# RWKV-7 attention and a hard-swish feed-forward on one core: whole-tile turns in place of half-tile turns

## The chip, the core and the metric

The kernel runs on one core of one Trainium2 chip. Its engines work side by side, each through its own queue in order: TensorE (PE for the matmuls, PEld for the loads of weights), VectorE (DVE), ScalarE (ACT), GpSimd (POOL) and SyncE (SP), which issues most of the DMAs. Matmuls write to PSUM, which the program here uses in eight banks of 512 fp32 columns by 128 partitions; DVE and ACT move results on to SBUF ("eviction"). The metric is device time in microseconds, the median of the runs. Lower is better.

## What is computed

First a recurrence with a state of 40 x 40 per head, for 4 batches, 8 heads, 768 steps; then its output, as 3072 rows of 320, goes through a feed-forward block with 2048 inner features. All of it is fp32.

```python
for t in range(S):                       # S = 768, D = 40
    y[:, :, t] = einsum('bhd,bhde->bhe', rt, state)
    Sa = einsum('bhde,bhe->bhd', state, at)
    state_decay = state * wt[:, :, None, :] - einsum('bhd,bhe->bhde', Sa, bt)
    state = state_decay + einsum('bhd,bhe->bhde', vt, kt)
# x = y as (B*S, H*D) = (3072, 320)
h = x @ w_in                             # (320, 2048)
g = h * clip(h + 3.0, 0.0, 6.0) / 6.0
return g @ w_out                         # (2048, 320)
```

## The kernel before

**Units.** The sequence is cut into blocks of 64 steps. A unit is one block of two batches with all 8 heads: its two batches lie on the two halves of the 128 partitions. There are 24 units in 6 groups of four. Within a block the recurrence is written as matrix products: A and B scaled by running products of the decays ("gam") and their inverses ("rgam"), a 64 x 64 triangular matrix F per head and batch, its inverse ("tinv"), and products with the state.

**Stages of a unit.** `prepare(i)` holds what needs no state: `w_stage` and `gam_stage` (running products of W and their inverses), `a_stage` and `b_stage` (A and B turned and scaled), `F`, `k_stage`, `factor_stage` (the inverse gammas turned back, with which K and B are scaled in their own layout), `e_stage`, `ev_stage`. `step(i)` holds the rest: `s_RT` and `s_VT` (R and V turned), `s_R`, `s_C`, `s_S` (the state turned), `s_U`, `s_UT`, `s_rS`, `s_sn` (the sums added to the state), `s_H`, `s_y`, and the moves of y into the layout of the feed-forward.

**Turns.** Inputs arrive with time on the partitions and are wanted with features there. A turn is a TensorE transpose: the data is the loaded weight, the identity is streamed through. `turn_pairs` (L416) turns a tensor in four transposes of 128 x 128 into one PSUM bank. `turn_halves` (L425) does it in eight transposes of 64 x 128, one for each half of the partitions and pair of heads. Each streams 64 columns of the identity, the two halves of the array work at the same time, and the results of the two halves lie in two banks, half a bank each; a second tensor shares these banks. The evictions then come in two instructions, one for each bank, over which `in_halves` and `parts_of` run. The flag `halves` chooses: it is set for units 8 to 23 in `prepare` (A, B and the inverse gammas) and for units 4 to 23 in `step` (R and V). W, K and the state are always turned whole.

**Order.** The order of the instructions on every engine is written out by hand. After a part for the first two groups comes the main loop (from L1280) over units 4 to 23. Each unit has four blocks; block m runs the stages that the lists `OWN_STAGES`, `AHEAD_STAGES` and `CLOSE_STAGES` set for the unit itself and for the one being prepared ahead (units 8 to 23, mostly five units ahead). Between the blocks, `feed` puts pieces of the feed-forward (`expand`, L961, and `contract`, L984) and steps of the inversion of F (`invert`, on DVE).

Inside a block `together` first issues the TensorE work of all stages in the order of the list `PRODUCTS`, then all evictions in the order of `RESULTS`, which also decides when the loads for later units are issued on SP. It counts banks: five are there for this work, and where the next product would need a sixth it closes the group early. A stage in `TURNS` takes a bank of its own; the others share pairs of banks while they have columns left.

```python
PRODUCTS = ["W", "S", "K", "RT", "VT", "A", "B", "factor",
            "y", "EV", "R", "C", "U", "UT", "rS", "sn", "H", "E", "F"]
TURNS = PRODUCTS[:3]
```

So in a typical unit the four blocks hold, on TensorE: W, RT, VT, y (of the unit before), EV; then S, A, B, R, C; then K, U, UT, rS, F; then factor, sn, H, E.

Of the kernel before, what the change touches and what calls it, by code (L numbers as in the profile page):

```python
# [11 lines left out]
ALU = mybir.AluOpType  # L12
AF = mybir.ActivationFunctionType
# [3 lines left out]
P = 128  # L17
BL = 64
HB = BL // 2
L = 32  # L20
SLOT = 64


def _ap(ap, extra, dims):

    return bass.AP(tensor=ap.tensor, offset=ap.offset + extra, ap=[list(ap.ap[0])] + dims)
# [3 lines left out]
def kernel(  # L30
# [42 lines left out]
    nc = tc.nc  # L73
    B, H, T, D = r.shape
    NG = T // (2 * BL)
    NPR = H // 2
    NP = B // 2
    NU = 2 * NP
# [16 lines left out]
    def bank(tag, shape, bufs):  # L95
        return ps.tile(shape, F32, name=tag, tag=tag, bufs=bufs)
# [3 lines left out]
    def ps_any(shape):  # L100
        tag, bufs = ring[0]
        ring.rotate(-1)
        return bank(tag, shape, bufs)
# [4 lines left out]
    def ps_pair(*dims):  # L108

        n = 1  # L110
        for d in dims:
            n *= d
        if shared[0] is None or shared[1] + n > 512:
            shared[:] = [ps_any([P, 512]) for _ in range(2)], 0
        at = shared[1]
        shared[1] += n
        views, step = [], n
        for d in dims:
            step //= d
            views.append([step, d])  # L120
        return [_ap(t[:], at, views) for t in shared[0]]
# [4 lines left out]
    ident = const.tile([P, P], F32, name="ident")  # L126
    nc.gpsimd.affine_select(
        out=ident[:], in_=ones, pattern=[[1, P]],
# [4 lines left out]
        out=ones[:, 0:BL], in_=ones[:, 0:BL], pattern=[[1, BL]],  # L133
# [3 lines left out]
        out=ones[BL:P, 0:BL], in_=ones[BL:P, BL:P], pattern=[[1, BL]],  # L137
# [271 lines left out]
    def following(i):  # L409

        if i < 2 * NU:

            return i + 2 if i % NU < NU - 2 or i % 2 == 0 else None
        return i + 1

    def turn_pairs(x):  # L416

        o = ps_any([P, NPR, P])
        for n in range(NPR):
            nc.tensor.transpose(out=o[:, n, :],  # L420
                                in_=x[:, 2 * n:2 * n + 2, :].rearrange("p s e -> p (s e)"),
                                identity=ident[:])
        return o

    def turn_halves(x):  # L425

        o = ps_pair(NPR, BL)
        for n in range(NPR):
            for q in range(2):
                nc.tensor.transpose(out=o[q][:, n, :],  # L430
                                    in_=x[half(q), 2 * n:2 * n + 2, :].rearrange("p s e -> p (s e)"),
                                    identity=ident[half(q), half(q)])
        return o

    def in_halves(x):
        return [x[:, :, half(q)] for q in range(2)]

    def turn_in(x, halves):

        return turn_halves(x) if halves else [turn_pairs(x)[:]]  # L440

    def parts_of(x, halves):
        return in_halves(x) if halves else [x[:]]

    def turned(name):
        return tmp.tile([P, NPR, P], F32, name=name, tag="turned", bufs=5)

    def half(i, n=SLOT):
        return slice(SLOT * i, SLOT * i + n)
# [20 lines left out]

    def prepare(i, F):
        n, o = i % NU, data[i]
        halves = i >= 2 * NU
        def w_stage():
            wt = turn_pairs(o["WN"])
            yield PE
# [27 lines left out]
            yield from ()  # L504

        def a_stage():
            x = turn_in(o["AN"], halves)
            yield PE
            rv = o["rg"][:].rearrange("p r (q i) -> p (r q) i", q=2)
            nc.vector.reciprocal(rv[:, :, HB:BL], o["prods"][:, :, 1, 1:HB + 1])  # L510
            at = o["at"] = grp.tile([P, NPR, P], F32, name="at", tag="at")
            for y, z, g in zip(parts_of(at, halves), x, parts_of(o["G"], halves)):
                nc.vector.tensor_tensor(out=y, in0=z, in1=g, op=ALU.mult)
            fetch("A", following(i))

        def b_stage():
            x = turn_in(o["BN"], halves)
            yield PE
            bt = o["bt"] = turned("bt")
            for y, z, g in zip(parts_of(bt, halves), x, parts_of(o["rg"], halves)):  # L520
                nc.vector.tensor_tensor(out=y, in0=z, in1=g, op=ALU.mult)

        def f_by_32():

# [38 lines left out]

        def factor_stage():

            if halves:
                rg = ps_pair(NPR, SLOT)
                for pr in range(NPR):
                    for s in range(2):
                        nc.tensor.transpose(out=rg[s][:, pr, :], in_=o["rg"][half(s), pr, :],  # L570
                                            identity=ident[half(s), half(s)])
            else:
                rg = ps_any([P, NPR, P])
                for pr in range(NPR):
                    nc.tensor.transpose(out=rg[:, pr, :], in_=o["rg"][:, pr, :], identity=ident[:])
            yield PE
            rgt = tmp.tile([P, H, D], F32, name="rgt", bufs=RGT)
            if halves:
                for s in range(2):
                    nc.scalar.activation(out=rgt[:, s::2], in_=rg[s][:, :, 0:D], func=AF.Copy)  # L580
            else:
                nc.scalar.activation(
                    out=rgt[:], in_=rg[:].rearrange("p r (s e) -> p (r s) e", s=2)[:, :, 0:D],
                    func=AF.Copy,
                )
            t = grp.tile([P, HD + WPAD], F32, name="KBt", tag="KBt", bufs=NU + 2)
            nc.gpsimd.memset(t[:, 2 * HD:], 0.0)
            for x, name in enumerate("KB"):
                o[name] = t[:, x * HD:x * HD + WPAD]
                nc.gpsimd.tensor_tensor(  # L590
                    out=o[name][:, 0:HD].rearrange("p (h e) -> p h e", h=H),
                    in0=o[name + "N"][:, :, 0:D], in1=rgt[:], op=ALU.mult,
                )
            if i > 2 * NU:
                fetch("V", i)
            for name in "BK":
                fetch(name, following(i))
# [137 lines left out]
    def step(i):  # L735

        n, o = i % NU, data[i]
        g, p = names[i]
        st, dec, VN = state[p], o["dec"], o["VN"]
        fresh = i < NP  # L740
        halves = i >= NU
        m = {}

        def s_RT():
            x = turn_in(o["RN"], halves)
            yield PE
            m["RT"] = turned("RT")
            for y, z in zip(parts_of(m["RT"], halves), x):
                nc.scalar.activation(out=y, in_=z, func=AF.Copy)  # L749
            fetch("R", i + 1, nc.scalar if i == 0 else None)  # L750
            if fresh:
                nc.gpsimd.tensor_copy(last_dec[p][:], dec[:, 1])
                return
            scale = tmp.tile([P, 2, NPR], F32, name="scale", bufs=2)
            nc.gpsimd.tensor_tensor(out=scale[:], in0=last_dec[p][:], in1=dec[:, 0], op=ALU.mult)
            nc.gpsimd.tensor_copy(last_dec[p][:], dec[:, 1])
            nc.vector.tensor_tensor(out=st[:, :, :, 0:D], in0=st[:, :, :, 0:D],
                                    in1=_ap(scale[:], 0, [[NPR, 2], [1, NPR], [0, D]]), op=ALU.mult)
# [16 lines left out]
                nc.vector.tensor_tensor(out=R[:, s], in0=rp[s], in1=o["EV"][:, s], op=ALU.add)  # L775

        def s_VT():
            x = turn_in(VN, halves)
            yield PE
            m["VT"] = turned("VT")  # L780
            for y, z in zip(parts_of(m["VT"], halves), x):
                nc.scalar.activation(out=y, in_=z, func=AF.Copy)

        def new_U():
            U = m["U"] = grp.tile([P, H, SLOT], F32, name="U", tag="U", bufs=1)
# [323 lines left out]
    n, cleared = 0, []  # L1109
# [48 lines left out]
    for line in PLAN:  # L1158
        plan.append([])
        while line:  # L1160
            i = line.popleft()
            if i != "T":
                i = int(i)
# [30 lines left out]
    for _ in range(18):  # L1194
# [10 lines left out]
    CLOSE_STAGES = [["W", "gam"], ["A", "B"], ["F", "K", "factor"], ["E"], ["EV"]]  # L1205


    PRODUCTS = ["W", "S", "K", "RT", "VT", "A", "B", "factor",
                "y", "EV", "R", "C", "U", "UT", "rS", "sn", "H", "E", "F"]
    RESULTS = ["RT", "y", "W", "gam", "VT", "EV", "R", "S", "C", "A", "B", "move", "move2",  # L1210
               "U", "UT", "rS", "F", "K", "sn", "H", "E", "factor"]
    TURNS = PRODUCTS[:3]
    WIDTH = {"R": NPR * D, "U": NPR * D, "sn": NPR * D, "EV": NPR * D}
    BLOCKS = 4

    def together(stages):
# [10 lines left out]

        for name in PRODUCTS:
            for stage in stages.get(name, []):
                if name in TURNS:  # L1230
                    need = 1
# [3 lines left out]
                if banks + need > 5:  # L1235
                    finish()
                    banks, need = 0, 1 if name in TURNS else 2
                banks += need
                rest = stage()
                next(rest)  # L1240
                begun.append((name, rest))
        begun.extend((name, stage()) for name in stages if name not in PRODUCTS
                     for stage in stages[name])
# [35 lines left out]
    m = 0  # L1279
# [59 lines left out]
```

## Time and profile before

| | |
|---|---|
| median of 3 runs | 840.49 us (839.77 to 842.09) |
| the profiled execution | 842.09 us |
| its span, first to last instruction | 840.4 us |
| TensorE matmul busy | 753.9 us (90%) |
| TensorE weight loads busy | 635.5 us (76%) |
| DVE / ACT / POOL busy | 549.1 / 322.6 / 158.2 us |
| granted TensorE clock, mean of the span | 0.937 |
| L992 and L968, the feed-forward's products | 234.6 and 198.1 us |
| half turns at L430 and L570 | 39.0 us in 704 instructions |

Busy times are of one execution. In rows of the timeline the first number is the start, the second the time from the first start to the last end of the group; matmuls overlap their followers, so the time that a group takes from TensorE is read from its start to the next group's start. "ident,R" in such a row names the streamed operand and then the weight; "64\*128" is the shape of the weight, "128x64" or "64x64" that of the streamed one. In rows of groups the number after the bar is the busy time in us and the mean of one instruction in ns, and after the next bar the idle time of the engine just before them.

### The profile page before, as it was taken

How to read it: one execution, taken by the hardware profiler on the slowest of the kernel's cores; microseconds unless marked ns; L12 is line 12 of the kernel's file. 1: busy time of each engine (PE TensorE's matmuls, PEld its weight loads, DVE VectorE, ACT ScalarE, POOL GpSimd, SP SyncE). 2: the span in 40 equal slices, each digit the busy share in tenths (PEclk: the TensorE clock that was granted, in tenths of full speed). 3: DMA queues.
4: the chain of work that ended last, by engine and by line, in shares of the span. 5: the costliest groups of instructions: out<-in, count | busy, mean ns of one | idle time of the engine just before them, and what ended most of it. 6: DMA issues, size and time to landing. Idle time of an engine off the chain costs nothing.

```text
span 840.4 us, 35835 instructions
## 1 busy us (share of the span) xinstructions
PE 753.9 (90%) x15832; PEld 635.5 (76%) x15832; DVE 549.1 (65%) x1112; ACT 322.6 (38%) x868; POOL 158.2 (19%) x307
## 2 busy tenths in 40 slices
PE   4722866898999998999999999999999999999998
PEld 3622766686877877888888888888888888888886
DVE  6989597887865769855589744699556675232211
ACT  1322654232265533454433545334553324322111
POOL 3231310222112230312230322022122102000000
PEclk9755576999999998999999999999999999999999
DMA  7573343331033331232321332231232101110000
GB/s 140 83 176 92 90 105 91 69 68 34 9 59 59 63 61 28 43 55 46 61 44 33 59 59 44 44 57 29 47 64 43 24 22 28 25 23 15 16 19 16
DMA packets 174218, 45.05 MB, mean 54 GB/s; under 512 B 157424, under 2 KB 172784, under 8 KB 174064
## 3 DMA queue, kind: packets, MB, share of 16 engines
q1 hardware_dynamic: 171920, 42.44, 25.7%
q8 instruction: 125, 2.05, 1.0%
q10 hardware_dynamic: 2144, 0.33, 0.2%
q14 instruction: 29, 0.24, 0.1%
HBM read 34.08 MB, written 3.93 MB: 45 GB/s over the span
## 4 chain that ended last, share of the span: by engine, by line
PE 73%; DVE 12%; issue 6%; ACT 2%; POOL 2%; DMA 2%; SPq 0%; POOLq 0%; DVEq 0%; ACTq 0%
PE o L992 23%; PE h L968 20%; PE h L973 5%; PE any L458 4%; PE any L888 3%; PE any L420 2%; PE any L430 2%; PE any L864 2%; PE any L770 1%; DVE prod L660 1%; PE any L809 1%; DVE parts L320 1%; DVE x L666 1%; PE any L830 1%; DVE score L467 1%
## 5 line engine op out<-in xcount | busy, mean ns | idle before, releaser
L992 PE MATMUL o<-wout,gt 128*128 128x320 f32 x768 | 234.6, 449 | 0.0
L968 PE MATMUL h<-xt,win 128*128 128x128 f32 x1536 | 198.1, 283 | 5.0 <-DVE gt L979 5.0
L968 PEld LDWEIGHTS h<-xt,win 128*128 128x128 f32 x1536 | 186.7, 196 | 13.9 <-DVE gt L979 5.7
L992 PEld LDWEIGHTS o<-wout,gt 128*128 128x128 f32 x768 | 139.3, 191 | 54.4 <-issue 1.4
L979 DVE SCALAR_TENSOR_TENSOR gt<-gt,h 128x512 f32<-128x512 f32 x96 | 61.3, 681 | 87.1 <-ACT gt L978 87.0
L978 ACT ACTIVATE gt<-h,three 128x512 f32<-128x512 f32 x96 | 60.8, 684 | 108.3 <-PE h L973 108.2
L903 POOL TENSOR_TENSOR yg<-ys,gam 128x512 f32<-128x512 f32 x24 | 41.4, 1726 | 182.9 <-DVE ys L900 125.5
L660 DVE TENSOR_TENSOR prod<-x 128x30 f32<-128x30 f32 (+9 forms) x180 | 61.9, 344 | 13.5 <-POOL x L651 8.1
L590 POOL TENSOR_TENSOR KBt<-K,rgt 128x320 f32<-128x320 f32 x24 | 21.2, 882 | 248.2 <-ACT rgt L580 213.2
L666 DVE TENSOR_TENSOR x<-x,prod 128x30 f32<-128x30 f32 (+9 forms) x180 | 63.3, 352 | 5.2
L873 DVE TENSOR_TENSOR state<-any,state 40x160 f32<-40x160 f32 x96 | 30.9, 321 | 47.5 <-PE any L458 26.0
L973 PE MATMUL h<-xt,win 64*128 64x128 f32 x768 | 55.8, 285 | 0.0
L467 DVE COPY_PREDICATED score<-mask,any 128x256 f32<-128x256 int32 x143 | 53.4, 437 | 1.7 <-PE any L458 1.1
L973 PEld LDWEIGHTS h<-xt,win 64*128 64x128 f32 x768 | 46.6, 187 | 5.2 <-issue 0.3
L495 DVE RECIPROCAL gam<-prods 128x256 f32<-128x256 f32 x24 | 41.5, 1741 | 13.4 <-POOL yg L903 12.1
L510 DVE RECIPROCAL rgam<-prods 128x256 f32<-128x256 f32 x24 | 41.8, 1741 | 0.0
L484 DVE TENSOR_TENSOR_SCAN prods<-wm,start 128x528 f32<-128x528 f32 x24 | 30.1, 1254 | 17.5 <-ACT wm L481 15.8
L623 ACT ACTIVATE EV<-any 64x160 f32<-64x160 f32 x92 | 24.9, 297 | 43.0 <-PE any L617 34.7
L888 PE MATMUL any<-score,KBt 64*64 64x64 f32 x1536 | 31.8, 233 | 3.5 <-DVE score L467 2.1
L888 PEld LDWEIGHTS any<-score,KBt 64*64 64x64 f32 x1536 | 27.9, 145 | 6.4 <-issue 2.4
L900 DVE TENSOR_TENSOR ys<-any,ys 128x256 f32<-128x256 f32 x44 | 16.6, 419 | 24.4 <-PE any L617 12.6
L749 ACT ACTIVATE RT<-any 128x256 f32<-128x256 f32 (+1 forms) x44 | 15.5, 401 | 42.4 <-PE any L430 42.4
(195 smaller groups left out, 1107.2 us busy)
## 6 DMA issues: line engine op xcount, KB each, us to landing
B<-in_b_dram SPq DMA_DIRECT2D x48, 80.0 KB
K<-in_k_dram SPq DMA_DIRECT2D x48, 80.0 KB
V<-in_v_dram SPq DMA_DIRECT2D x96, 40.0 KB
out_dram<-ob SPq DMA_DIRECT2D x48, 80.0 KB
R<-in_r_dram SPq DMA_DIRECT2D x92, 40.0 KB
W<-in_w_dram SPq DMA_DIRECT2D x40, 80.0 KB
A<-in_a_dram SPq DMA_DIRECT2D x40, 80.0 KB
xt<-yg SPq DMA_DIRECT2D x72, 40.0 KB
```

The costliest lines, as they stand in the source:

```text
L467: nc.vector.copy_predicated(out=x[:, 4 * i:4 * i + 4, :], mask=mask4, data=o[i])
L495: nc.vector.reciprocal(gv[:, :, 0:HB], o["prods"][:, :, 0, 1:HB + 1][:, :, ::-1])
L510: nc.vector.reciprocal(rv[:, :, HB:BL], o["prods"][:, :, 1, 1:HB + 1])
L660: nc.vector.tensor_tensor(out=pv, in0=_ap(x[:], (i + 1) * L + i, [[L, n], [0, i]]), in1=_ap(x[:], i * L, [[0, n], [1, i]]), op=ALU.mult,)
L666: nc.vector.tensor_tensor(out=rest, in0=rest, in1=pv, op=ALU.add)
L888: nc.tensor.matmul(out=y[q][half(s), pr, :], lhsT=o[name][half(q), h * D:h * D + SLOT], rhs=m[name][half(q), 4 * rs + 2 * s + j, :], start ...
L903: nc.gpsimd.tensor_tensor(out=yg[:], in0=m["ys"][:].rearrange("p r q t -> p r (q t)"), in1=o["G"][:], op=ALU.mult)
L968: nc.tensor.matmul(out=hp[c][:, i, :], lhsT=win[:, t, j * P:(j + 1) * P], rhs=xt[:, t, :], start=(t == 0 and i == 0), stop=False)
L973: nc.tensor.matmul(out=hp[c][:, i, :], lhsT=win2[half(c), (j0 + i) * P:(j0 + i + 1) * P], rhs=xt[half(c), 2, :], start=False, stop=(i == N ...
L978: nc.scalar.activation(out=gt[:], in_=hp[c][:], func=AF.Relu, bias=three[:], scale=1.0)
L979: nc.vector.scalar_tensor_tensor(out=gt[:], in0=gt[:], scalar=6.0, in1=hp[c][:], op0=ALU.min, op1=ALU.mult)
L992: nc.tensor.matmul(out=op[:], lhsT=gts[c][:, n, :], rhs=wout[:, c * HJ + r * NQ + n, :], start=((split or r == 0) and c == 0 and n == 0), ...
```

## The change

The half turns go. A, B, R, V and the inverse gammas of all units are turned by four transposes of 128 x 128 each, in one bank, and evicted by one instruction. `turn_halves`, `in_halves`, `turn_in`, `parts_of` and the flag `halves` are taken out. In the list of products RT and VT come ahead of W, and A and B ahead of K; the first eight names, not three, are turns with a bank of their own. The order of evictions and of loads, the stages of the blocks and the feed-forward stay.

```diff
-    def turn_halves(x):
-        o = ps_pair(NPR, BL)
-        for n in range(NPR):
-            for q in range(2):
-                nc.tensor.transpose(out=o[q][:, n, :],
-                                    in_=x[half(q), 2 * n:2 * n + 2, :].rearrange("p s e -> p (s e)"),
-                                    identity=ident[half(q), half(q)])
-        return o
...
-    def turn_in(x, halves):
-        return turn_halves(x) if halves else [turn_pairs(x)[:]]
...
         def a_stage():
-            x = turn_in(o["AN"], halves)
+            x = turn_pairs(o["AN"])
             yield PE
...
-            for y, z, g in zip(parts_of(at, halves), x, parts_of(o["G"], halves)):
-                nc.vector.tensor_tensor(out=y, in0=z, in1=g, op=ALU.mult)
+            nc.vector.tensor_tensor(out=at[:], in0=x[:], in1=o["G"][:], op=ALU.mult)
...
         def b_stage():
-            x = turn_in(o["BN"], halves)
+            x = turn_pairs(o["BN"])
...
-            for y, z, g in zip(parts_of(bt, halves), x, parts_of(o["rg"], halves)):
-                nc.vector.tensor_tensor(out=y, in0=z, in1=g, op=ALU.mult)
+            nc.vector.tensor_tensor(out=bt[:], in0=x[:], in1=o["rg"][:], op=ALU.mult)
...
         def factor_stage():
-            if halves:
-                rg = ps_pair(NPR, SLOT)
-                for pr in range(NPR):
-                    for s in range(2):
-                        nc.tensor.transpose(out=rg[s][:, pr, :], in_=o["rg"][half(s), pr, :],
-                                            identity=ident[half(s), half(s)])
-            else:
-                rg = ps_any([P, NPR, P])
-                for pr in range(NPR):
-                    nc.tensor.transpose(out=rg[:, pr, :], in_=o["rg"][:, pr, :], identity=ident[:])
+            rg = ps_any([P, NPR, P])
+            for pr in range(NPR):
+                nc.tensor.transpose(out=rg[:, pr, :], in_=o["rg"][:, pr, :], identity=ident[:])
...
-            if halves:
-                for s in range(2):
-                    nc.scalar.activation(out=rgt[:, s::2], in_=rg[s][:, :, 0:D], func=AF.Copy)
-            else:
-                nc.scalar.activation(
-                    out=rgt[:], in_=rg[:].rearrange("p r (s e) -> p (r s) e", s=2)[:, :, 0:D],
-                    func=AF.Copy,
-                )
+            nc.scalar.activation(
+                out=rgt[:], in_=rg[:].rearrange("p r (s e) -> p (r s) e", s=2)[:, :, 0:D],
+                func=AF.Copy,
+            )
...
         def s_RT():
-            x = turn_in(o["RN"], halves)
+            x = turn_pairs(o["RN"])
...
-            for y, z in zip(parts_of(m["RT"], halves), x):
-                nc.scalar.activation(out=y, in_=z, func=AF.Copy)
+            nc.scalar.activation(out=m["RT"][:], in_=x[:], func=AF.Copy)
...
         def s_VT():
-            x = turn_in(VN, halves)
+            x = turn_pairs(VN)
...
-            for y, z in zip(parts_of(m["VT"], halves), x):
-                nc.scalar.activation(out=y, in_=z, func=AF.Copy)
+            nc.scalar.activation(out=m["VT"][:], in_=x[:], func=AF.Copy)
...
-    PRODUCTS = ["W", "S", "K", "RT", "VT", "A", "B", "factor",
+    PRODUCTS = ["RT", "VT", "W", "S", "A", "B", "K", "factor",
                 "y", "EV", "R", "C", "U", "UT", "rS", "sn", "H", "E", "F"]
...
-    TURNS = PRODUCTS[:3]
+    TURNS = PRODUCTS[:8]
```

More of the change, by code (lines that the diff above doesn't have):

```diff
@@ L423, in turn_pairs @@
         return o
-    def turn_halves(x):
-        o = ps_pair(NPR, BL)
-        for n in range(NPR):
-            for q in range(2):
-                nc.tensor.transpose(out=o[q][:, n, :],
-                                    in_=x[half(q), 2 * n:2 * n + 2, :].rearrange("p s e -> p (s e)"),
-                                    identity=ident[half(q), half(q)])
-        return o
-    def in_halves(x):
-        return [x[:, :, half(q)] for q in range(2)]
-    def turn_in(x, halves):
-        return turn_halves(x) if halves else [turn_pairs(x)[:]]
-    def parts_of(x, halves):
-        return in_halves(x) if halves else [x[:]]
     def turned(name):
@@ L472, in prepare @@
         n, o = i % NU, data[i]
-        halves = i >= 2 * NU
         def w_stage():
@@ L740, in step @@
         fresh = i < NP
-        halves = i >= NU
         m = {}
         def s_RT():
-            x = turn_in(o["RN"], halves)
+            x = turn_pairs(o["RN"])
             yield PE
             m["RT"] = turned("RT")
-            for y, z in zip(parts_of(m["RT"], halves), x):
-                nc.scalar.activation(out=y, in_=z, func=AF.Copy)
+            nc.scalar.activation(out=m["RT"][:], in_=x[:], func=AF.Copy)
             fetch("R", i + 1, nc.scalar if i == 0 else None)
```

## The prediction

> **What bounds the kernel now.** I read the share of busy time first, then the slices, then busy time by stage, TensorE's waits, and last the order of its instructions.
>
> ```profile
> PE 753.9 (90%) x15832; PEld 635.5 (76%) x15832; DVE 549.1 (65%) x1112; ACT 322.6 (38%) x868; POOL 158.2 (19%) x307
> ...
> PE   4722866898999998999999999999999999999998
> ```
>
> ```profile
> 229.00:346.00 117.00, 110.78 (x2557) 92.25 (x2556) 83.58 (x176) 53.20 (x155) 23.00 (x49) 0.97 0.28 50
> 346.00:800.00 454.00, 452.99 (x10007) 383.15 (x10007) 270.13 (x574) 184.46 (x507) 84.48 (x145) 1.00 0.21 40
> ```
>
> The main loop, which holds every instruction that changes, starts at 229 us. The columns are the stretch, its length, busy time of PE, PEld, DVE, ACT and POOL, granted clock, DMA share and GB/s. From 346 us on TensorE idles 1.0 us in 454, so what the change does to TensorE's own time there goes into the total. Between 229 and 346 us there is some slack. The waits of TensorE from 229 us to the end:
>
> ```profile
> PE any L770 <- DVE score L467: 3.7, 1, 3.7
> PE h L968 <- DVE gt L979: 1.0, 1, 1.0
> PE any L549 <- ACT ys L853: 0.9, 1, 0.9
> PE any L458 <- issue: 0.8, 1, 0.8
> PE any L458 <- ACT UT L837: 0.5, 1, 0.5
> PE any L846 <- DVE score L467: 0.2, 1, 0.2
> ```
>
> That is 7.1 us, half of it in one place (315.7 to 319.4 us). Little else holds TensorE up, so what counts is how long a whole turn takes on TensorE against two half turns. Start to start, three stretches of its timeline tell:
>
> ```profile
> 250.72 0.60 PE L420 MATMUL any<-ident,W 128*128 128x128 f32 x4
> 251.15 1.24 PE L992 MATMUL o<-wout,gt 128*128 128x320 f32 x4
> ...
> 539.56 0.47 PE L570 MATMUL any<-ident,rgam 64*128 64x64 f32 x8
> 539.96 0.51 PE L864 MATMUL any<-V,KBt 64*40 64x40 f32 x32
> ...
> 547.80 0.60 PE L420 MATMUL any<-ident,W 128*128 128x128 f32 x4
> 548.34 0.46 PE L430 MATMUL any<-ident,R 64*128 64x64 f32 x8
> 548.63 0.41 PE L430 MATMUL any<-ident,V 64*128 64x64 f32 x8
> 548.98 1.16 PE L888 MATMUL any<-score,KBt 64*64 64x64 f32 x64
> ```
>
> Four whole turns (W) last 251.15 - 250.72 = 0.43 us when whole-array work follows, and 548.34 - 547.80 = 0.54 us when half-array work follows. So a border from whole to half costs about 0.10 us. Eight half turns last 0.29 (R, halves follow) or 0.35 us (V). The starts agree in all later units. I use 0.44 for a whole tensor, 0.30 + 0.34 for a pair of half tensors, 0.09 for a border.
>
> **The change, part by part.**
>
> *R and V of a unit* (20 units, 4 to 23). In 13 of them W is turned beside them: before 0.53 (W, border in it) + 0.30 + 0.34 = 1.17 us; after, three whole tensors and a border, 3 x 0.44 + 0.09 = 1.41. In 7 they stand alone: before 0.09 + 0.64 = 0.73, after 0.97. Both +0.24, so 20 x 0.24 = 4.8 us.
>
> *A and B* (16 units, 8 to 23), mostly behind the state's turn S, a whole-array one: the same sum, 16 x 0.24 = 3.8 us.
>
> *Inverse gammas* (16 units): before, border 0.09 + 0.40 (539.56 to 539.96) = 0.49; after 0.44 + 0.09 = 0.53. In four units K stands right ahead and the sum is the same. 16 x 0.045 = 0.7 us.
>
> Together TensorE gets 9.3 us more; with unrounded starts 9.6, which I take.
>
> The Trainium skill, "TensorEngine Tiling (Array Packing)", section Theoretical Speedup, gives a dimension of 64 or less up to 2x. It speaks against this change more strongly than the rows do. By that page whole turns would cost 0.60 where halves cost 0.30, some 0.30 for each of 72 tensors, or 21 us. The rows give 0.44 against 0.30 with borders counted, and the sum goes by them.
>
> *Evictions.* Two instructions become one in 56 places on ACT (RT, VT, rgt) and 32 on DVE (at, bt). The timeline has such pairs overlapped: RT 0.66, VT 0.69, rgt 0.50, at 0.69, bt 0.75 us. A single one, from the groups by form, is in the rows of the early units:
>
> ```profile
> L749 ACT ACTIVATE RT<-any 128x512 f32<-128x512 f32 x4 | 2.3, 586 | 0.0
> ```
>
> VT has 584 and rgt 432 ns there, at 625 and bt 682. So ACT saves 20 x 0.07 + 20 x 0.11 + 16 x 0.07 = 4.7 us, DVE 16 x 0.13 = 2.1 us. Both lie beside TensorE's work: 0. If TensorE's cover were gone, they would count in full.
>
> *Order.* RT and VT go ahead of W, A and B ahead of K. W's turn ends about 0.25 us later and its two ACT copies with it; in the unit at 518 us those copies end at 520.85 and the scan and reciprocal behind them take 1.25 + 1.75, while A's reciprocal, the next user, starts at 528.8. Every load is issued as often as before and in the same order on SP. That of W leaves up to 0.3 us later, that of R some 0.4 us earlier, and each has a unit (about 26 us) to land. POOL keeps its instructions. Price 0: TensorE's list of waits from 229 us on has no DMA in it. Were a load late, TensorE would stand for it.
>
> *PSUM.* A whole tensor takes one bank, where two half tensors shared two; the bank count of a block is the same but for the one with the inverse gammas (five instead of four). New neighbours: rS and F take the banks of A and B. In the unit at 518 us bt ends at 531.80 and rS starts at 532.38, 0.58 us clear, and the merged eviction is not slower. VT and W take banks that the state's sums and H leave: their last reader ends at 546.73 us where TensorE arrives at 547.80. I price this at 0, with bounds of 0 and, by the tightest row, 0.4 us in some 11 units (4.4 us) should bt come a whole microsecond later. No reason makes it a gain.
>
> *Stalls.* The 3.7 us wait at 315.7 us is for DVE, which runs there on a chain of its own from the F eviction at 302 us. TensorE arrives after one R/V and one A/B pair, 0.5 us later, so the wait is 3.2 us: -0.5. The 1.0 us wait at 557 us shrinks likewise by 0.25. At 279 us y lasts 1.54 us where it lasts 0.98 later: 0.56 goes to its wait for the bt eviction. It then needs the bank of A alone and comes 0.24 us later: -0.55. The 0.9 us wait at 243 us (F, for ys) becomes one of rS for UT at the same place: -0.2. Small ones: -0.1. What is late next in each is TensorE itself. Bounds: none of it shrinks (0), or all 7.1 us go. I take -1.6, since DVE's chains beyond these places stay.
>
> *Sum.* 9.6 - 1.6 = +8.0 us. The profiled execution took 842.09 us, its span 840.4 and 1.7 around; that makes 850.1. It was the slowest of three and stands 1.6 us above the median, so the median moves from 840.49 to **848.5 us**. A measurement of this kernel can tell about 0.3%, that is 2.5 us.
>
> **The clock.** Around the long wait:
>
> ```profile
> 315.00:318.40 3.40, 0.68 (x17) 0.54 (x16) 3.19 (x10) 0.67 (x2) 0.00 (x0) 1.00 0.32 66
> 318.40:321.80 3.40, 2.43 (x65) 2.27 (x66) 3.19 (x10) 0.00 (x0) 0.00 (x0) 0.50 0.39 82
> 321.80:325.20 3.40, 3.40 (x17) 3.40 (x18) 3.30 (x9) 0.00 (x0) 0.00 (x0) 0.50 0.11 24
> ```
>
> TensorE was busy 0.68 of 3.4 us, and the clock is at half for the 6.8 us after it. That costs 3.0 us: 24 matmuls of h took 4.58 instead of 2.7, the 64 small ones ahead of them 2.24 instead of 1.1. I leave this cost in, since a stretch with a fifth of work was enough.
>
> The skill's "TensorE: Matmul & The Clock Gate", Part 1, says that the clock falls after an idle window of about 3.4 us on a free-running grid. Read strictly, a wait of 3.2 us would not do it, and the total would be 845.5. The stretch above was not idle either and had the clock fall.
>
> **The rivals.**
>
> 1. *The half clock or more of the early waits goes* (the wait at 315 us falls on two stretches). For it: the wait gets shorter; against: 3.2 us still empties most of a stretch. 848.5 - 3.0 = 845.5, with 1 us more of waits 844.5.
>
> 2. *New bank waits*, rS for bt or VT for the masks. For it: 0.58 us of clearance in the tight units. Against: DVE has less to do and TensorE comes later. 4.4 us: 852.9.
>
> 3. *Faster: the evictions set the pace*, at the DVE and ACT queues in the loop. Then TensorE's 9.6 us would vanish in its waits and ACT's 4.7 us would be gained: 835.8. It decides if TensorE's waits from 229 us on are over 9.6 us; they are 7.1, with the 0.56 at y and 3.0 us of half clock 10.7, and every one would have to go to reach 839.4. From 346 us on, 27 of the 36 R/V and A/B pairs run with 1.0 us of waits, so this would need TensorE's busy time to hide waits that the profile does not show.
>
> 4. *Nothing changes*: whole turns cost no more than halves. The starts say otherwise; 840.5.
>
> **How the numbers follow.** My forecast (846.5 to 850.5) 0.74, the first rival 0.12, the second 0.09, the third 0.02, the fourth 0.03. The range takes in the first rival, and the second nearly to its end, with half a microsecond of scatter: 844.0 to 852.5; outside lie the third, the fourth and the ends. Slower by over 0.3% (above 843.0): 0.94; within: 0.04; faster: 0.02.
>
> **What would show it.** In the changed profile four turns of R, V, A, B and inverse gammas should each last 0.44 us start to start, and 0.53 ahead of half-array work; TensorE's busy time should rise by about 9.5 us; after 346 us its waits should stay near 1 us; the wait for the mask near 317 us should be about 3.2 us, with a half clock behind it. A whole turn under 0.35 us, or waits in every unit at L846 or at the turn of V, would make the forecast wrong.

## The result, and the profile after

The changed kernel takes 848.99 us (median of 4 runs, 848.88 to 849.13) where the kernel before takes 840.13 beside it (839.58 to 842.09): a ratio of 1.0101, 95% interval 1.0084 to 1.0119. It is slower by 8.86 us, and the forecast was 848.5. The profiled execution took 848.88 us, its span 847.2 and 1.7 around. Below, the lines of the changed kernel have numbers 20 to 37 lower than in the listing: L458 is L438, L467 is L447, L549 is L526, L575 (the whole turn of the inverse gammas) is L545, L617 is L583, L770 is L734, L837 is L800, L846 is L809, L864 is L827, L888 is L851, L968 is L931, L979 is L942, L992 is L955. L430 and L570 are gone, since all of A, B, R and V are turned at L420 and the inverse gammas at L545.

The page's busy times and TensorE's slices:

```profile
PE 763.3 (90%) x15480; PEld 648.0 (76%) x15480; DVE 549.3 (65%) x1080; ACT 318.3 (38%) x812; POOL 156.7 (18%) x307
...
PE   4623876898999989999999999999999999999997
```

TensorE is busy 9.4 us longer with 352 instructions fewer. ACT does 4.3 us less, and nothing of that shows in the time. By stage (the stretch, its length, busy PE, PEld, DVE, ACT and POOL, granted clock, DMA share, GB/s):

```profile
229.00:346.00 117.00, 111.76 (x2459) 93.77 (x2458) 83.03 (x166) 50.24 (x140) 21.22 (x45) 0.99 0.29 53
346.00:806.00 460.00, 457.41 (x9732) 390.17 (x9732) 270.06 (x551) 181.10 (x463) 83.07 (x145) 1.00 0.21 39
```

From 346 us on TensorE idles 2.6 us in 460, where it was 1.0 in 454, so nearly all that is added to it goes into the time. What holds it up from 229 us to the end (the waiting line, its releaser, us in all, times, longest):

```profile
PE any L734 <- DVE score L447: 3.2, 1, 3.2
PE h L931 <- DVE gt L942: 1.1, 1, 1.1
PE any L809 <- ACT UT L800: 0.8, 1, 0.8
PE any L809 <- issue: 0.6, 1, 0.6
PE any L526 <- issue: 0.6, 1, 0.6
PE any L583 <- issue: 0.5, 1, 0.5
PE any L438 <- ACT UT L800: 0.5, 1, 0.5
PE any L438 <- issue: 0.3, 1, 0.3
PE any L809 <- DVE score L447: 0.2, 1, 0.2
```

The wait for the mask went from 3.7 to 3.2, F's 0.9 for ys became 0.8 at rS, and the waits for which the profile shows no releaser ("issue") went from 0.8 to 2.0. After 346 us all waits together make 2.6 us, where the prediction expected them to stay near 1. The turns on TensorE's timeline (start, length of the group, form):

```profile
541.49 0.60 PE L545 MATMUL any<-ident,rgam 128*128 128x128 f32 x4
542.01 0.52 PE L827 MATMUL any<-V,KBt 64*40 64x40 f32 x32
...
549.80 0.60 PE L420 MATMUL any<-ident,R 128*128 128x128 f32 x4
550.24 0.60 PE L420 MATMUL any<-ident,V 128*128 128x128 f32 x4
550.68 0.60 PE L420 MATMUL any<-ident,W 128*128 128x128 f32 x4
551.21 1.16 PE L851 MATMUL any<-score,KBt 64*64 64x64 f32 x64
```

Start to start R and V take 0.44 us each, W and the inverse gammas, with half-array work behind them, 0.53 and 0.52. That is 1.41 us from R to y, where the kernel before took 1.18 for the same three tensors.

Behind the inverse gammas something changes that the prediction does not have. The next product of the feed-forward after them starts here, in the kernel before and in the changed one:

```profile
541.79 3.50 PE L992 MATMUL o<-wout,gt 128*128 128x320 f32 x12
...
543.79 3.50 PE L955 MATMUL o<-wout,gt 128*128 128x320 f32 x12
```

From the first turn of the inverse gammas to this start it is 2.23 us before (from 539.56) and 2.30 after (from 541.49), though the turn alone went from 0.40 to 0.52: the matmuls between give 0.05 us back. It is much the same in all 12 units in which these products follow, but for an issue wait in one. With the border of 0.09 us gone ahead of the turn, the inverse gammas cost TensorE nothing in these units. Where it comes from is seen (the last step of the matmuls of U and KBt is 0.08 us shorter, those of RT and UT 0.03 longer); why is not shown by any run.

Around the long wait:

```profile
312.66:316.07 3.41, 2.34 (x16) 1.75 (x14) 3.31 (x8) 1.03 (x2) 0.60 (x4) 1.00 0.48 87
316.07:319.49 3.42, 1.24 (x62) 1.12 (x64) 3.21 (x10) 0.00 (x0) 0.00 (x0) 1.00 0.45 93
319.49:322.90 3.41, 3.41 (x29) 3.30 (x22) 3.20 (x11) 0.00 (x0) 0.00 (x0) 0.50 0.12 30
322.90:326.31 3.41, 3.41 (x59) 3.12 (x60) 3.41 (x5) 1.09 (x4) 0.00 (x0) 1.00 0.04 10
```

The half clock (0.50) is still there, for one stretch of 3.4 us where it was two.

**Where the 8.9 us come from.** From the main loop's first turn (at 228.97 us before, at 226.89 after) to the end of the span it is 611.38 us before and 620.27 after, +8.89. The spans differ by 6.8 only, because the profiled execution of before was 2.1 us slower in the part ahead of the loop, in which both programs do the same. I cut the loop by TensorE's groups, start to start, each with the idle time behind it, and took the differences:

| tile | after less before, us |
|---|---|
| R, V | +2.79, +2.52 |
| A, B | +2.20, +2.52 (B without the long wait behind it +2.98) |
| inverse gammas | +2.19 |
| the state's turn, K, W: a border less behind them | -1.23, -0.38, -0.17 |
| h, o of the feed-forward: a border less, h also clock | -1.23, -0.81 |
| rS, EV: waits there, in part moved from F and from the matmuls of RT and UT (-0.24, -0.25) | +1.71, +1.01 |
| y; the matmuls of U and KBt; of RT and VT | -0.45; -0.95; -0.44 |

With B at +2.98 and, of h and o, only the 22 borders ahead of turns (-2.07), the first five rows make +8.8: R and V 4.5, A and B 3.7, the inverse gammas 0.7. The matmuls behind the inverse gammas take 0.7 off again (U and KBt -0.95, RT and UT +0.3), so TensorE's own work makes +8.1. Waits and clock make the remaining +0.8: the long wait -0.46, the half clock -0.9, y -0.45, F and rS at 242 us -0.1; against that four issue waits (at 275, 369, 631 and 742 us) where there was one (at 273), whose steps together are longer by 2.0 us, the wait for gt and the tail behind the last product +0.3, and half a microsecond in groups of tenths that I did not place. Start to start such a step is longer than the wait in it (0.80 us for the 0.58 at 742 us), since the wait is counted from the end of the matmul ahead.

### The profile page after: what moved, and what is told of

Read it like the earlier page. It is cut to its first block, busy times and chain, and to the rows that moved or that the text cites. A ratio compares the mean times of both kernels' runs of the same rounds, so it can differ in the third digit from the quotient of the medians.

```text
span 847.2 us, 35021 instructions
## 1 busy us (share of the span) xinstructions
PE 763.3 (90%) x15480; PEld 648.0 (76%) x15480; DVE 549.3 (65%) x1080; ACT 318.3 (38%) x812; POOL 156.7 (18%) x307
## 4 chain that ended last, share of the span: by engine, by line
PE 76%; DVE 12%; issue 4%; SPq 3%; ACT 2%; POOL 2%; DMA 1%; DVEq 0%; POOLq 0%; ACTq 0%
PE o L955 24%; PE h L931 21%; PE any L420 6%; PE h L936 5%; PE any L438 4%; PE any L851 3%; PE any L827 2%; DVE prod L626 1%; PE any L772 1%; PE any L734 1%; DVE x L632 1%; PE any L793 1%; PE any L583 1%; PE any L809 1%; DVE gam L474 1%
## 5 line engine op out<-in xcount | busy, mean ns | idle before, releaser
L955 PE MATMUL o<-wout,gt 128*128 128x320 f32 x768 | 234.2, 448 | 0.0
L931 PE MATMUL h<-xt,win 128*128 128x128 f32 x1536 | 198.9, 284 | 5.1 <-DVE gt L942 5.1
L931 PEld LDWEIGHTS h<-xt,win 128*128 128x128 f32 x1536 | 187.3, 197 | 14.3 <-DVE gt L942 6.3
L955 PEld LDWEIGHTS o<-wout,gt 128*128 128x128 f32 x768 | 139.1, 191 | 54.3 <-issue 1.2
L942 DVE SCALAR_TENSOR_TENSOR gt<-gt,h 128x512 f32<-128x512 f32 x96 | 61.3, 680 | 86.7 <-ACT gt L941 86.6
L626 DVE TENSOR_TENSOR prod<-x 128x30 f32<-128x30 f32 (+9 forms) x180 | 64.5, 358 | 13.4 <-POOL x L617 8.1
L447 DVE COPY_PREDICATED score<-mask,any 128x256 f32<-128x256 int32 x143 | 53.4, 436 | 1.4 <-PE any L438 1.0
L713 ACT ACTIVATE RT<-any 128x512 f32<-128x512 f32 x24 | 14.3, 594 | 57.2 <-PE any L420 57.2
L851 PE MATMUL any<-score,KBt 64*64 64x64 f32 x1536 | 31.8, 235 | 3.4 <-DVE score L447 2.2
L851 PEld LDWEIGHTS any<-score,KBt 64*64 64x64 f32 x1536 | 28.1, 147 | 8.0 <-issue 4.5
```

The lines of the kernel that those rows point to most:

```text
L447: nc.vector.copy_predicated(out=x[:, 4 * i:4 * i + 4, :], mask=mask4, data=o[i])
L626: nc.vector.tensor_tensor(out=pv, in0=_ap(x[:], (i + 1) * L + i, [[L, n], [0, i]]), in1=_ap(x[:], i * L, [[0, n], [1, i]]), op=ALU.mult,)
L851: nc.tensor.matmul(out=y[q][half(s), pr, :], lhsT=o[name][half(q), h * D:h * D + SLOT], rhs=m[name][half(q), 4 * rs + 2 * s + j, :], start ...
L931: nc.tensor.matmul(out=hp[c][:, i, :], lhsT=win[:, t, j * P:(j + 1) * P], rhs=xt[:, t, :], start=(t == 0 and i == 0), stop=False)
L942: nc.vector.scalar_tensor_tensor(out=gt[:], in0=gt[:], scalar=6.0, in1=hp[c][:], op0=ALU.min, op1=ALU.mult)
L955: nc.tensor.matmul(out=op[:], lhsT=gts[c][:, n, :], rhs=wout[:, c * HJ + r * NQ + n, :], start=((split or r == 0) and c == 0 and n == 0), ...
```

## The experiments

Each has its median beside that of the kernel before on the same chip, and the length of the loop by its profile, against 611.38 us before and 620.27 after.

### R and V alone

```diff
-        halves = i >= NU
+        halves = False                     # in step: R and V
-    PRODUCTS = ["W", "S", "K", "RT", "VT", "A", "B", "factor",
+    PRODUCTS = ["RT", "VT", "W", "S", "K", "A", "B", "factor",
-    TURNS = PRODUCTS[:3]
+    TURNS = PRODUCTS[:5]
```

> The kernel before with R and V alone turned whole (one eviction each), A, B and the inverse gammas in halves. My theory (what a turn takes on TensorE sets the total): 20 x 0.24 = 4.8 us more, less 0.5 for waits that shrink, so 844.4 us against 840.1. Rival (the evictions set the pace): forty ACT instructions fewer, so no loss or a gain of some 3 us, 837 to 840. Rival (waits for banks): a loss far from 4.8 us, with waits at V or y in every unit.

845.4 us against 840.62, a ratio of 1.006 (1.0047 to 1.0073). The loop takes 615.23 us, +3.85, in an execution that was the fastest of the five (843.07). R +2.79 and V +2.52 as in the full change, the seven borders ahead of R -0.66, W -0.16: +4.5 on TensorE. The long wait shrank to 3.45 us, the half clock behind it lasts one stretch instead of two (-0.9), and issue waits added 0.4. Of the rivals neither shows: there is no gain, and no wait at V or y.

### A and B alone

```diff
-            x = turn_in(o["AN"], halves)
+            x = turn_in(o["AN"], False)     # and B, at, bt alike
-    PRODUCTS = ["W", "S", "K", "RT", "VT", "A", "B", "factor",
+    PRODUCTS = ["W", "S", "A", "B", "K", "RT", "VT", "factor",
-    TURNS = PRODUCTS[:3]
+    TURNS = PRODUCTS[:5]
```

> The kernel before with A and B alone turned whole. My theory: 16 x 0.24 = 3.8 us more, less 0.25 at the long wait near 316 us and 0.55 ahead of y at 279 us, so 843.1 us; with e1 and 0.7 us for the inverse gammas this has to make up the whole change. Rival (evictions): 840.1 less 2 us. Rival (waits for banks): waits of rS for bt in the units where it has 0.58 us of clearance, up to 4 us on top, 847.

844.14 us, a ratio of 1.004 (1.0027 to 1.0053). The loop takes 615.78 us, +4.40. A +2.20, B +2.75 with the wait behind it (3.69 to 3.45, so +2.99 without), the state's turn -1.23, three borders in h and o -0.28: +3.7. The median is 1.0 us above the forecast; y gained 0.3 us of the 0.55, and an issue wait of 0.46 us stands right behind. rS waits nowhere for bt. So the two parts alone make 3.85 + 4.40 = 8.25 us of the loop's 8.89. The inverse gammas were not changed alone; what they cost is read from the full change.

### The new order with half turns

```diff
-    PRODUCTS = ["W", "S", "K", "RT", "VT", "A", "B", "factor",
+    PRODUCTS = ["RT", "VT", "W", "S", "A", "B", "K", "factor",
-    TURNS = PRODUCTS[:3]
+    TURNS = ["W", "S", "K"]
```

> The kernel before with all half turns kept and only the list of products in the new order (R and V ahead of W, A and B ahead of K). My theory: W now stands between half turns and half-array products, so each of 13 units has one more border between whole and half, 13 x 0.09 = 1.2 us, 841.3 us. Rival (the order and its bank waits make the loss): up to the whole 8.9 us, 849.

842.75 us, a ratio of 1.0026 (1.0016 to 1.0036), and the loop 613.60, +2.2. TensorE's timeline of this kernel shows why:

```profile
544.69 2.84 PE L968 MATMUL h<-xt,win 128*128 128x128 f32 x24
547.46 0.47 PE L430 MATMUL any<-ident,R 64*128 64x64 f32 x8
547.76 0.41 PE L430 MATMUL any<-ident,V 64*128 64x64 f32 x8
548.10 0.66 PE L420 MATMUL any<-ident,W 128*128 128x128 f32 x4
548.69 1.16 PE L888 MATMUL any<-score,KBt 64*64 64x64 f32 x64
```

The 24 matmuls of h last 2.77 us to the next start where half turns follow, and 2.67 (547.13 to 549.80) in the changed kernel where whole ones do. W lasts 0.59 where it lasted 0.54. A whole W between half-array groups so costs 0.10 + 0.05 = 0.15 us more in 12 of the 13 units (in one o follows it); by tiles it is 1.7 us of the 2.2, where the theory, without the 0.05, had 1.2. The rest lies in issue waits and small places. No bank wait came that could be put down to the order. With whole turns what stands ahead of W is whole.

### The evictions in two instructions again

The changed kernel, with every single eviction of at, bt, RT, VT and the inverse gammas split in two, those of units 0 to 7 too: ACT's instructions go from 812 to 884, DVE's from 1080 to 1128.

```diff
-            nc.scalar.activation(out=m["RT"][:], in_=x[:], func=AF.Copy)
+            for q in range(2):              # and VT, at, bt, the inverse gammas
+                nc.scalar.activation(out=m["RT"][:, :, half(q)], in_=x[:, :, half(q)], func=AF.Copy)
```

> The changed kernel with each of the 88 merged evictions split in two again, out of the one bank. My theory: they lie beside TensorE, 0 to 0.3 us, so 849.0 us. Rival (evictions count): ACT's 4.7 and DVE's 2.1 us come on top, up to 856.

850.88 us, a ratio of 1.011 (1.009 to 1.013). Busy times of the page, and TensorE's waits in the loop:

```profile
PE 764.3 (90%) x15480; PEld 649.0 (77%) x15480; DVE 552.9 (65%) x1128; ACT 322.0 (38%) x884; POOL 156.9 (19%) x307
```

```profile
PE any L737 <- DVE score L447: 3.2, 1, 3.2
PE h L935 <- DVE gt L946: 1.1, 1, 1.1
PE any L813 <- ACT UT L804: 0.8, 1, 0.8
PE any L585 <- issue: 0.5, 1, 0.5
PE any L438 <- ACT UT L804: 0.5, 1, 0.5
PE h L940 <- issue: 0.3, 1, 0.3
PE any L813 <- DVE score L447: 0.2, 1, 0.2
```

ACT and DVE work 3.7 and 3.6 us more, and TensorE's waits for them are those of the changed kernel. The loop takes 618.66 us, 1.6 less than 620.27, of which 1.1 are issue waits that are not there. So inside the loop of this execution the saved evictions are worth nothing, and the part ahead of it (226.49 us) is no longer than in the changed kernel (226.89). But this execution took 846.86 us, one of two near 846.7; the other four took 850.2 to 851.8 and have no trace. The median is 1.9 us above the 848.99, and the two ratios' intervals overlap: a cost of up to that much is not excluded by the times.

### The changed kernel again, and with the work ahead of the long wait put off

The long wait has DVE behind it: just ahead of it nine steps of the inversion of F are issued with the first feed of block 0 of unit 7. Here they stay out of that feed and come later.

```diff
-            feed(rate / 2, inversion)
+            feed(rate / 2, 0 if i == 2 * NU - 1 and j == 0 else inversion)
```

> The changed kernel once more, beside the three that follow. 849.0 us; its stretch from the first turn of the main loop to the end 620 us, as before. It stands here to read the next kernel and the split evictions against.

848.89 us, a ratio of 1.01 (1.0083 to 1.0117); the loop 620.04, with issue waits of 1.4 us at two of the four places above (near 275 and 741 us).

> The changed kernel, but the nine steps of the inversion that DVE does between the two parts of one block (unit 7, first block) are left to the later places. My theory: the long wait of TensorE for the mask near 318 us is made by these steps; they last some 0.3 us each, so the wait falls from 3.2 to about 0.7 us, and with it the half clock goes (some 2 us): 849.0 - 4.5 = 844.5 us. Rival (a clock that falls only after a whole idle window of 3.4 us would not have cost anything here): 849.0 - 2.5 = 846.5. Rival (DVE's steps come back as a wait in a later block): 849.

849.94 us, a ratio of 1.0109 (1.0091 to 1.0127). My theory fell, and the rival that the steps come back as a wait held; the loop takes 621.56 us. Waits, and the stretches around the new one:

```profile
PE h L931 <- DVE gt L942: 3.6, 2, 2.3
...
PE any L662 <- ACT RT L713: 0.5, 1, 0.5
...
PE any L734 <- DVE score L447: 0.4, 1, 0.4
PE any L662 <- ACT wm L460: 0.3, 1, 0.3
```

```profile
341.55:344.96 3.41, 1.10 (x8) 0.77 (x7) 3.37 (x9) 0.00 (x0) 0.00 (x0) 1.00 0.31 51
344.96:348.37 3.41, 3.41 (x27) 3.08 (x28) 3.12 (x9) 0.00 (x0) 0.00 (x0) 0.50 0.00 0
```

The wait at 316 us is 0.4, and no half clock follows it. But DVE is as late at 344 us: a gate of the feed-forward (gt) is waited for 2.3 us, and the half clock comes there.

### The kernel before with the same work put off

The same edit in the kernel before, first alone and then with one more: unit 8 no longer has its inverse gammas turned in a crowded block.

```diff
-            ahead[u, m] = prepared(u), CLOSE_STAGES if close else AHEAD_STAGES
+            ahead[u, m] = prepared(u), CLOSE_STAGES if close and u > 2 * NU else AHEAD_STAGES
```

> The kernel before with the same nine steps left to later places. My theory: 3.7 us of wait becomes about 1.2, and 3 us of half clock go: 840.6 - 5.5 = 835.1 us, so that the price of the whole turns against it would be the full 9 to 9.6 us of TensorE's time. Rival (the steps come back as a wait): 840.6.

843.15 us, a ratio of 1.0027 (1.0014 to 1.004): slower, where the theory had 835.1.

```profile
PE any L696 <- ACT wm L481: 2.8, 1, 2.8
PE any L549 <- ACT ys L853: 0.9, 1, 0.9
PE h L968 <- DVE gt L979: 0.9, 1, 0.9
PE any L770 <- DVE score L467: 0.8, 1, 0.8
```

The wait went from 315 to 350 us, to the third block of the inverse, and half clock for three stretches (10 us) followed it. ACT's copy of W ends it, but ACT itself had stood there for 5.5 us until DVE's turn of the inverse (tb) was done at 346.5 us. The 0.8 us that are left of the wait at 315 us still have one stretch of half clock behind them.

> As the one before, and the inverse gammas of unit 8 are turned one block later, so that the products of its third block fit in five banks and the group isn't closed early. My theory: F's wait of 0.94 us for the eviction of ys at 243 us goes, 834.2 us. Rival: it turns up elsewhere, 835.1.

840.9 us, a ratio of 1.0004 (0.9994 to 1.0014), where the theory had 834.2. F's wait of 0.94 us for ys is gone, the 2.9 us at the third block stay, and a gate is waited for 1.2 us at 340 us.

### The steps spread

The second edit of the kernel before alone, and then with the nine steps neither in one heap ahead of the wait nor at the end, but three each in the next three feeds.

```diff
-            feed(rate / 2, inversion)
+            feed(rate / 2, 0 if i == 2 * NU - 1 and j == 0 else inversion + (i == 2 * NU - 1 and j == 1))
...
-            feed(rate / 2, inversion)
+            feed(rate / 2, inversion + (i == 2 * NU - 1 and j < 2))
```

> The kernel before, with the inverse gammas of unit 8 turned back one block later, as in most units. In the kernel of the eighth run, which also had this, the 0.94 us wait of TensorE at 243 us (F, for ys) was gone. If that wait goes by this edit alone, the stretch from the main loop's first turn is 610.4 us instead of 611.4 and the median 839.3. Rival: the wait comes back one product later, or in other waits of DVE and ACT between 243 and 300 us: 840.2, no change.

839.98 us against 840.43, a ratio of 0.9994 (0.9985 to 1.0003). F's wait at 243 us is gone, and the loop takes 610.78. But issue waits of 0.3 us at 259 and at 263 us are there that the kernel before did not have, and the median lies nearer to the rival's 840.2 than to 839.3; the times can't tell the two apart.

> The kernel before, with that change of unit 8, and the nine steps of the inversion that were issued ahead of the long wait at 315 us now issued three at a time in the next three feeds (four in place of three beside each product of the feed-forward), that is some 5 to 25 us later, and not at the end of the list. Theory, that the wait of 2.8 us at 349 us in the seventh and eighth run came only because the nine steps were the last to be done: that wait is gone, the one at 315 us stays at about 0.8, and of the half clock one stretch is left at most; 611.4 - 2.85 - 0.94 - 1 = 606.6 us in the loop, and a median of 835.5. Rival, that DVE has no room for these steps anywhere between 315 and 350 us: waits of 2 to 3 us come back for DVE, at the gates of the feed-forward or at the third block near 349 us, the loop is 610 to 612 us and the median 839 to 841.

838.59 us, a ratio of 0.998 (0.9972 to 0.9989), and the loop 609.55: between the two theories, nearer to the rival.

```profile
PE h L968 <- DVE gt L979: 3.2, 3, 1.7
PE any L617 <- issue: 1.0, 2, 0.7
PE any L770 <- DVE score L467: 0.8, 1, 0.8
PE any L696 <- ACT wm L481: 0.4, 1, 0.4
```

```profile
312.31:315.72 3.41, 2.55 (x81) 2.23 (x78) 3.21 (x11) 0.30 (x1) 0.00 (x0) 1.00 0.39 78
339.61:343.03 3.42, 1.73 (x7) 0.95 (x6) 3.33 (x10) 1.76 (x4) 1.68 (x2) 1.00 0.00 0
343.03:346.44 3.41, 3.41 (x124) 3.17 (x123) 3.41 (x3) 1.12 (x2) 1.01 (x1) 1.00 0.31 53
```

One wait of 3.7 us became four of 0.4 to 1.7 at 313, 329, 343 and 349 us, with nearly the same sum (0.84 + 0.60 + 1.69 + 0.45 = 3.58). What went is the half clock: none of these is followed by one. In the three orders tried DVE is what limits this part; its busy time is 3.1 to 3.4 us of every 3.4 in the rows above. This kernel is the fastest of those here: 1.8 us (0.2%) below the kernel before, 1.4 below the run ahead, whose interval it just touches.

## Why the prediction was right, point by point

- *Whole turns cost 0.44 us, 0.53 ahead of half-array work.* Right: 0.44, 0.53, 0.52 in the rows above, in all five tensors.
- *R and V 4.8 us, A and B 3.8, inverse gammas 0.7, together 9.6 unrounded.* Measured by tile 4.5, 3.7 and 0.7, together 8.8. The parts held; but they sum to 9.3, unrounded starts give about 9.2, and the 9.6 that was taken does not follow from them. And the sum put the matmuls behind the inverse gammas at nothing, without a word: they gave 0.7 us back, so TensorE's own work grew by 8.1. The rule of the Trainium skill that I had weighed against the rows ("TensorEngine Tiling (Array Packing)", Theoretical Speedup: up to 2x for a dimension of 64 or less) would have made it 21 us by my estimate for 72 of the 88 tensors. The runs have 0.44 against 0.30 for a turn, 1.5x.
- *Evictions 0.* Right in the loop as far as it was traced: split again, they change none of TensorE's waits (fourth experiment). ACT's busy time fell by 4.3 of the 4.7 us forecast; DVE's did not fall by 2.1 but stayed (549.1 and 549.3), which cost nothing either.
- *Order 0.* Right for this change, by the sum alone: the parts make up the total without it. With half turns the same order costs 2.2 us, 1.7 of it borders and W's step between halves (third experiment).
- *PSUM 0.* Right: no wait for bt at rS and none of VT or W in the list of waits; rS waits for UT once, as forecast for F's wait, and for "issue".
- *Stalls -1.6.* This is the term that was mis-sized most. What it named it had right: the long wait gave 0.46 of 0.5, y 0.45 of 0.55, F's wait 0.18 of 0.2. The wait for gt at 560 us did not shrink by 0.25 but grew from 1.0 to 1.1. What it had not is issue waits, which went from 0.8 to 2.0 and whose steps make +2.0; they differ between two executions of the same kernel (1.9 and 1.4 us in all), so part of that belongs to the execution and not to the change.
- *The half clock stays in, 3.0 us.* It is there, but about 2.1: the 24 matmuls of h behind the wait took 4.37 us (4.58 before, 2.67 elsewhere), the small ones ahead of them 1.51 (2.24 before, 1.1 elsewhere). So 0.9 us came off here that the prediction left in.
- *The sum, +8.0.* TensorE's own work was priced 1.5 us too high (9.6 against 8.1), and waits and clock 2.4 too low (-1.6 against +0.8). The two errors are opposite, so that the loop's 8.9 and a median of 848.99 against 848.5 look better than the terms: the mechanism, the price of a whole turn on a full TensorE, is shown, but the half microsecond is in part luck.
- *What is late next is TensorE itself.* Right for the change. Where I took the same wait away, it did not hold: DVE was late next, at 344 us (sixth run), or ACT behind DVE near 350 us (seventh and eighth).

The rivals: the half clock went in no run of the changed kernel as it stands. No new bank wait showed. The evictions set no pace, and whole turns are dearer than halves.

## What to carry to other kernels

Where TensorE is full, read a replaced form's price from start to start of its groups, with the border to the next shape in it, and multiply by the count: here that came to 8.8 us where the loop grew by 8.9, while the instructions saved on the other engines gave nothing that the traces show. That the two numbers are so near is chance: behind the turns 0.7 us came off at the next groups, and 0.8 us of waits and clock came on at others. Read on to the next group that both kernels share, not only to the end of the turn. Before a wait is taken away, look at how full the releasing engine is from there on: DVE was busy some 94% or more of the changed kernel's stretches around the wait, so a wait moved off one place came back at the next. What could still be gained was the clock, by cutting one long gap into short ones: 1.4 to 1.8 us here.

## What the runs showed of the hardware that I had not expected

- The clock falls after stretches that are far from idle. The half clock lasts 3.41, 6.83 or 10.24 us in these traces, that is one, two or three stretches. In the stretch ahead of it TensorE was busy 0.71 us in the kernel before (half clock for two stretches after), 1.24 in the changed one (one), 1.10 in the sixth run (one) and 0.65 in the seventh (three). The Trainium skill's "TensorE: Matmul & The Clock Gate", Part 1, speaks of an idle window of some 3.4 us on a free-running grid; no stretch here was wholly idle, and the measurement decides. But no busy time of a single stretch sorts the cases: half clock came after 1.73 us in the fourth run and not after 1.73 in the last, and after 2.55 in the seventh run (both below) and not after 2.55 in the last (whose stretches are counted back from the one fall that it has, at 834.5 us). What else decides stays open; where in a stretch the gap lies was not varied.

```profile
315.86:319.27 3.41, 1.73 (x67) 1.54 (x68) 3.18 (x10) 0.00 (x0) 0.00 (x0) 1.00 0.34 72
319.27:322.68 3.41, 3.41 (x19) 3.41 (x18) 3.26 (x10) 0.00 (x0) 0.00 (x0) 0.50 0.13 33
...
312.91:316.33 3.42, 2.55 (x84) 2.06 (x83) 3.28 (x10) 0.95 (x2) 0.00 (x0) 1.00 0.37 75
316.33:319.74 3.41, 3.41 (x17) 3.41 (x17) 3.27 (x10) 0.00 (x0) 0.00 (x0) 0.50 0.39 82
```

- A border from whole to half costs about the same whatever stands ahead of it: 0.10 us at h (2.77 against 2.67), 0.09 at o (1.28 against 1.19, ahead of the inverse gammas near 540 us), 0.09 at a whole turn (0.53 against 0.44). A whole W with half turns ahead of it and half-array work behind it took another 0.05 (0.59 against 0.54).
- TensorE's waits that the profile shows no releaser for ("issue", 0.3 to 2.3 us in all in the loops of these profiles) differ in size and in part in place: one lies between 270 and 281 us in all twelve profiles, the others come and go. An account of single microseconds has to leave room for them.
